# A transformer block on one core: scores in one block ahead of V, tiled half chunks, and two transposes moved from TensorE to DMA

## The chip, the core and the metric

The kernel runs on one core of a Trainium2 chip. The metric is the device time of one execution in microseconds; smaller is better. The core has five engines with queues of their own: TensorE (PE) for matrix products, VectorE (DVE) and ScalarE (ACT) for everything element by element, GpSimd (POOL), and SyncE (SP), which here issues nearly all DMA transfers. Each engine works through its instructions in order; they wait for each other by semaphores.

## The reference, cut to what matters

One diffusion-transformer block: B = 2 sequences of N = 256 tokens, D = 1152 features, two heads of Dh = 576, an MLP of F = 4608.

```python
mod = (silu(c) @ w_mod).reshape(B, 6, 1, D)
shift_a, scale_a, gate_a, shift_m, scale_m, gate_m = [mod[:, i] for i in range(6)]
h = layernorm(x) * (1 + scale_a) + shift_a
q, k, v = (h @ wqkv) split into three, each in H = 2 heads of 576
attn = softmax(q @ k.T * 576 ** -0.5)          # per sequence and head
x = x + gate_a * ((attn @ v) @ wo)
h2 = layernorm(x) * (1 + scale_m) + shift_m
return x + gate_m * (gelu(h2 @ w_fc1) @ w_fc2)
```

## The kernel before

All matrix operands are bf16 and are cut into chunks of 128 rows: D is nine chunks (KD = 9), the 512 tokens are four token tiles t = 0 to 3 (two for each sequence b). A head has 576 = 4.5 chunks, so chunk 4 (HC = 4) is shared: its first 64 rows (HP = 64) belong to head 0, its last 64 to head 1.

The order on each engine is the order in which the program issues its instructions; a loop at its end (L762) pins it. The stages are K, Q, scores and V together, the attention product (PV), the output projection with the second layer norm (Wo), the first MLP product (F1) and the second (F2).

- **Weights.** Every weight matrix of 1152 x 1152 takes one slot of a pool of five (wide, bufs=5), so a load waits until an earlier matrix has been used for the last time. SyncE issues all loads, in program order, mostly in three pieces of 864 KB. In the order of issue: w_scale_a and w_k, w_shift_a, w_q, w_gate_a, w_v, w_shift_m, w_scale_m, w_o, w_f1[0] and w_f1[1] (L121 to L130), then w_f1[2], w_f1[3] and w_gate_mT, the last with three DMA transposes from DRAM (L530 to L537), and during F1 the four parts of w_f2 (L673).
- **Gates.** gate_natural (L410) multiplies silu(c) with w_gate_a during Q (after m = 6), writes the row to DRAM and reads it back with GpSimd's queue, broadcast over the partitions. vec_section makes shift_m and scale_m as columns during V.
- **PSUM.** Accumulators take one of six banks (acc_tile), small results one of two others (aux_tile). `evac` copies a bank to SBUF, in turn on VectorE and ScalarE.
- **Scores.** score_tile (L473) makes one tile of 128 queries by 256 keys in a bank of its own with five matmuls. The shared chunk is multiplied in full: kT4m holds K's chunk 4 twice, each time with the other head's 64 rows set to zero, and v4m does the same for V. reduce_max, Exp with a row sum, reciprocal and a multiplication follow; each of the eight tiles comes ahead of one of the first eight of V's twelve groups (v_group, L503), and its normalization after it.
- **PV.** The attention weights are transposed by 16 TensorE transposes into PSUM (pTt, L546) and copied to SBUF. Then each of nine chunks of each sequence is made by two matmuls, the shared one by four (L567), and copied into aT.
- **Wo and LN2.** wo_group (L629) makes 128 tokens by 384 features, VectorE multiplies with gate_a (tmp), GpSimd adds x into x1, ln2_stats gathers the statistics one group later, and ln2_normalize gives xn2 in bf16 when a token tile is complete. The normalized tiles of a sequence are transposed by 18 TensorE transposes (pt, L605), and on the way out of PSUM VectorE or ScalarE multiply by scale_m and add shift_m into hT. These pieces of work are strewn between other matmuls by `filler`: those of sequence 0 into the last Wo groups, those of sequence 1 into F1.
- **F1** computes m = 0 to 9 for sequence 0, then for sequence 1 (180 matmuls of 256 columns), so that it can begin before sequence 1 is normalized, then m = 10 to 35 for both at once. After m = 14, dot_section makes gate_m with 18 VectorE instructions from w_gate_mT.
- **F2** multiplies 36 chunks for each of 12 groups, VectorE multiplies with gate_m and GpSimd adds x1.

The lines that the steps below speak of:

```python
if m == 6:                                        # L456, in the loop over q
    gate_a = gate_natural(0, w_gate_a)
...
nc.tensor.transpose(                              # L546
    pTt[:, kc, qt * P:(qt + 1) * P],
    attn_tiles[(b, h, qt)][:, kc * P:(kc + 1) * P], ident[:],
)
...
if (t, i) == (3, 0):                              # L654, in the loop over Wo groups
    fill_ln2(0, 5)
```

Of the kernel before, what the change touches and what calls it, by code (L numbers as in the profile page):

```python
# [19 lines left out]
def kernel(  # L20
# [11 lines left out]
    nc = tc.nc  # L32
# [76 lines left out]
    def load_section(name, s):  # L109
        w = wide_tile(name)  # L110
        for r in range(0, KD, 3):
            nc.sync.dma_start(w[:, r:r + 3, :], wmod_v[:, r:r + 3, s * D:(s + 1) * D])
        return w
# [9 lines left out]
    w_gate_a = load_section("w_gate_a", S_GATE_A)  # L123
    w_v = load_panels("w_v", wqkv_v, 2 * D)
    w_shift_m = load_section("w_shift_m", S_SHIFT_M)
    w_scale_m = load_section("w_scale_m", S_SCALE_M)
    w_o = load_panels("w_o", wo_v, 0)
    w_f1 = [None] * 4
    w_f1[0] = load_panels("w_f1_0", wfc1_v, 0)
    w_f1[1] = load_panels("w_f1_1", wfc1_v, D)  # L130
# [10 lines left out]
    kT4m = act.tile([P, H, T], BF16, name="kT4m")  # L141
    v4m = act.tile([P, NT, H, P], BF16, name="v4m")
    nc.gpsimd.memset(kT4m[HP:P, 0, :], 0.0)
    nc.gpsimd.memset(kT4m[0:HP, 1, :], 0.0)
    nc.gpsimd.memset(v4m[:, :, 0, HP:P], 0.0)
    nc.gpsimd.memset(v4m[:, :, 1, 0:HP], 0.0)

# [138 lines left out]
    def k_evac(m):  # L288
        if m == HC:
            evac(kT4m[0:HP, 0, :], pk[m][0:HP, :])  # L290
            evac(kT4m[HP:P, 1, :], pk[m][HP:P, :])
        else:
            evac(kT[:, m, :], pk[m][:])
# [157 lines left out]
    for m in range(KD):  # L451
# [7 lines left out]
        if m == 6:  # L459
            gate_a = gate_natural(0, w_gate_a)  # L460


    def head_chunks(h):
        return list(range(HC + 1)) if h == 0 else list(range(HC, KD))
# [5 lines left out]
    attnT_all = soft[:, 3 * n_s * N:4 * n_s * N].rearrange("p (i c n) -> p i c n", c=TPB, n=N)  # L470
    attn_tiles = {}

    def score_tile(b, h, qt):  # L473
        chunks = head_chunks(h)
        q0 = b * N + qt * P
        ps_s = acc_tile([P, N], "ps_s")
        for i, cc in enumerate(chunks):
            if cc == HC:
                k_ap = kT4m[:, h, b * N:(b + 1) * N]
            else:  # L480
                k_ap = kT[:, cc, b * N:(b + 1) * N]
            nc.tensor.matmul(  # L482
                ps_s[:], qT[:, cc, q0:q0 + P], k_ap,
                start=(i == 0), stop=(i == len(chunks) - 1),
            )
        negmax = small.tile([P, 1], FP32, name="negmax", tag="negmax")
        nc.vector.reduce_max(negmax[:], ps_s[:], axis=AX.X, negate=True)
        si = (b * H + h) * TPB + qt
        e_sb = e_all[:, si, :]
        rowsum = small.tile([P, 1], FP32, name="rowsum", tag="rowsum")  # L490
        nc.scalar.activation(e_sb, ps_s[:], ACT.Exp, bias=negmax[:], scale=1.0, accum_out=rowsum[:])
        attn = attn_all[:, si, :]
        attn_tiles[(b, h, qt)] = attn

        def finish():
            rs = small.tile([P, 1], FP32, name="rs", tag="rs")
            nc.vector.reciprocal(rs[:], rowsum[:])
            nc.vector.tensor_scalar_mul(attn, e_sb, rs[:])

        return finish  # L500


    def v_group(pnl, t):  # L503
# [7 lines left out]
        c4 = HC * P - pnl * PW  # L511
        if 0 <= c4 and c4 + P <= PW:
            evac(v4m[:, t, 0, 0:HP], pacc[:, c4:c4 + HP])
            evac(v4m[:, t, 1, HP:P], pacc[:, c4 + HP:c4 + P])

    score_order = [(b, h, qt) for b in range(B) for h in range(H) for qt in range(TPB)]
    v_order = [(pnl, t) for pnl in range(NPD) for t in range(NT)]
    shift_m = scale_m = None
    for i, (pnl, t) in enumerate(v_order):
        fin = score_tile(*score_order[i]) if i < len(score_order) else None  # L520
        v_group(pnl, t)
        if fin is not None:
            fin()
        if i == 8:
            shift_m = vec_section(sT, w_shift_m, "shift_m")
        if i == 10:
            scale_m = vec_section(sT, w_scale_m, "scale_m")
            nc.vector.tensor_scalar_add(scale_m[:, :, 0:B], scale_m[:, :, 0:B], 1.0)

    w_f1[2] = load_panels("w_f1_2", wfc1_v, 2 * D)  # L530
    w_f1[3] = load_panels("w_f1_3", wfc1_v, 3 * D)
    w_gate_mT = wide_tile("w_gate_mT")
    for r in range(0, KD, 3):
        nc.sync.dma_start_transpose(
            w_gate_mT[:, :, r * P:(r + 3) * P],
            w_mod[r * P:(r + 3) * P, S_GATE_M * D:(S_GATE_M + 1) * D],
        )  # L537


    attnTs = {}  # L540
    for b in range(B):
        for h in range(H):
            pTt = acc_tile([P, TPB, N], "pTt", BF16)
            for qt in range(TPB):
                for kc in range(TPB):
                    nc.tensor.transpose(  # L546
                        pTt[:, kc, qt * P:(qt + 1) * P],
                        attn_tiles[(b, h, qt)][:, kc * P:(kc + 1) * P], ident[:],
                    )
            attnT = attnT_all[:, b * H + h, :, :]  # L550
            evac(attnT, pTt[:])
            attnTs[(b, h)] = attnT

    cpairs = [(0, 1), (2, 3), (4, 5), (6, 7), (8,)]
    for b in range(B):
# [247 lines left out]
```

## Time and profile before

| What | Value |
|---|---|
| median of five runs | 249.05 us (248.59 to 249.12) |
| the profiled execution | 249.12 us |
| its span | 247.3 us |
| granted TensorE clock | 1.0 throughout |
| bytes moved by DMA | 52.18 MB, mean 211 GB/s over the span |
| Q begins, scores and V begin | 33.98 us, 52.77 us |
| pTt transposes begin, PV begins | 77.33 us, 78.23 us |
| Wo begins, F1 begins | 82.76 us, 101.15 us |
| F1 ends, F2 begins | 173.62 us |

A profile is one execution; its span runs from its first to its last recorded instruction, and what lies around the span makes the difference to the execution's time. Times in the trace count from the span's start. In the chain of waits each piece is either work of an engine or a wait, followed back from the last instruction: what stands there is on the path that sets the end. In the rows, L is a line of the kernel above, PE the matmuls, PEld the weight loads that overlap them, SPq the issuing of transfers by SyncE. A number after x is a count of instructions, and the arrow in "out<-in" points from what is read to what is written. Several program tiles share one name in the trace: "big" holds q, k, v and the attention output, "soft" the softmax's three arrays, and "w_f" all parts of the MLP weights.

### The profile page before, as it was taken

To read this page: it belongs to the slowest core of one execution; us is meant where nothing else is said; L and a number is where in the kernel's file an instruction comes from. 1 tells how busy PE (TensorE), PEld (TensorE's weight loads), DVE (VectorE), ACT (ScalarE), POOL (GpSimd) and SP (SyncE) were. 2 spreads that over 40 slices of the span, in tenths; PEclk is the share of its full clock that TensorE was granted. 3 is DMA by queue.
4 is the path that set the end of the run, shared out by engine and by line. 5 is a ranking of instruction groups with operands and counts; after the bars stand their busy time and mean duration, and the time that the engine had idled before them with its cause. 6 is when DMAs were issued, how large, how long until landed. Compare 5 with 4: busy or idle time off the path is not lost.

```text
span 247.3 us, 4011 instructions
## 1 busy us (share of the span) xinstructions
PE 238.7 (97%) x1709; PEld 144.2 (58%) x1709; DVE 88.3 (36%) x209; ACT 68.3 (28%) x133; POOL 34.4 (14%) x53
## 2 busy tenths in 40 slices
PE   6799999999999999989999999999999999999994
PEld 2485444456667766878844444444566666666674
DVE  2761471335544677821099991000011100000001
ACT  6632341153424424593332223322000000000000
POOL 4000021031000166300000003100011122111111
PEclk9999999999999999999999999999999999999999
DMA  6999999999999999999793007999500000000000
GB/s 222 325 333 362 367 330 372 336 362 392 381 328 329 327 328 327 327 292 241 145 321 103 0 3 222 326 342 326 170 16 16 19 16 16 21 16 16 30 21 16
DMA packets 63837, 52.18 MB, mean 211 GB/s; under 512 B 12091, under 2 KB 58571, under 8 KB 63819
## 3 DMA queue, kind: packets, MB, share of 16 engines
q1 hardware_dynamic: 62928, 50.14, 67.0%
q0 software_dynamic: 864, 1.79, 2.1%
q8 instruction: 13, 0.21, 0.4%
q14 instruction: 5, 0.04, 0.1%
q10 hardware_dynamic: 27, 0.00, 0.0%
HBM read 48.08 MB, written 1.19 MB: 199 GB/s over the span
## 4 chain that ended last, share of the span: by engine, by line
PE 90%; DMA 3%; DVE 2%; ACT 2%; issue 1%; SPq 0%; ACTq 0%; DVEq 0%
PE pacc L748 28%; PE pacc L681 26%; PE pacc L506 7%; PE pacc L454 7%; PE pacc L634 7%; PE pk L265 4%; DMA w_scale_a<-in_w_mod_dram 3%; PE pk L298 2%; PE pa L567 2%; PE ps_s L482 2%; PE pn L381 1%; DVE stats L175 1%; PE pt L605 1%; PE pm L233 1%; PE pt L243 1%
## 5 line engine op out<-in xcount | busy, mean ns | idle before, releaser
L681 PE MATMUL pacc<-hT,w_f 128*128 128x512 bf16 (+1 forms) x414 | 71.1, 333 | 0.0
L748 PE MATMUL pacc<-w_f,gT 128*128 128x384 bf16 (+2 forms) x468 | 70.5, 314 | 0.0
L748 PEld LDWEIGHTS <-gT 128*128 128x128 bf16 x468 | 44.4, 98 | 26.2
L681 PEld LDWEIGHTS <-w_f 128*128 128x128 bf16 x414 | 40.3, 98 | 29.4
L754 DVE TENSOR_TENSOR tmp<-pacc,gate 128x384 f32<-128x384 f32 (+2 forms) x13 | 6.8, 526 | 88.3 <-PE pacc L748 88.3
L445 DVE SCALAR_TENSOR_TENSOR late<-w_gate_mT,late 128x1152 bf16<-128x1152 bf16 x18 | 24.4, 1357 | 12.1 <-DMA w_gate_mT<-in_w_mod_dram 11.5
L725 ACT ACTIVATE gT<-pacc 128x512 bf16<-128x512 f32 x26 | 15.5, 597 | 35.0 <-PE pacc L681 35.0
L756 POOL TENSOR_TENSOR o_sb<-tmp,x 128x384 bf16<-128x384 f32 (+1 forms) x12 | 11.7, 972 | 73.3 <-DVE tmp L754 73.3
L506 PE MATMUL pacc<-w_v,hT 128*128 128x384 bf16 x108 | 19.2, 326 | 0.0
L634 PE MATMUL pacc<-w_o,big 128*128 128x384 bf16 x108 | 18.5, 326 | 0.0
L454 PE MATMUL pacc<-hT,w_q 128*128 128x512 bf16 x81 | 17.8, 379 | 0.0
L641 POOL TENSOR_TENSOR x<-tmp,x_sb 128x384 f32<-128x384 f32 x11 | 10.1, 915 | 33.3 <-issue 27.2
L506 PEld LDWEIGHTS <-hT 128*128 128x128 bf16 x108 | 10.4, 98 | 6.3 <-issue 0.5
L634 PEld LDWEIGHTS <-big 128*128 128x128 bf16 x108 | 10.4, 98 | 6.2
L265 PE MATMUL pk<-big,w_k 128*128 128x256 bf16 (+2 forms) x90 | 13.4, 293 | 0.4 <-ACT big L252 0.4
L454 PEld LDWEIGHTS <-w_q 128*128 128x128 bf16 x81 | 7.8, 98 | 9.6 <-issue 0.3
L265 PEld LDWEIGHTS <-w_k 128*128 128x128 bf16 x90 | 7.5, 97 | 3.4 <-DMA w_k<-in_wqkv_dram 0.3
L436 POOL DMA_DIRECT2D gates_dram<-grow x4 | 2.0, 513 | 45.2 <-DVE grow L711 45.2
L284 DVE TENSOR_SCALAR big<-pacc 128x512 bf16<-128x512 f32 x5 | 3.5, 691 | 13.3 <-PE pacc L454 13.3
L640 DVE TENSOR_TENSOR tmp<-pacc,gate 128x384 f32<-128x384 f32 x12 | 6.7, 556 | 3.7 <-PE pacc L634 3.6
L697 ACT ACTIVATE gT<-pacc 128x512 bf16<-128x512 f32 x10 | 5.9, 598 | 7.4 <-PE pacc L681 7.4
L158 PE MATMUL pwarm<-zeros 128*128 128x512 bf16 x19 | 6.5, 486 | 1.2 <-DVE eps_t L92 1.2
(109 smaller groups left out, 171.3 us busy)
## 6 DMA issues: line engine op xcount, KB each, us to landing
w_f<-in_w_fc_dram SPq DMA_DIRECT2D x14, 864.0 KB, 10.2
w_f<-in_w_fc_dram SPq DMA_DIRECT2D x2, 2592.0 KB, 18.4
w_f<-in_w_fc_dram SPq DMA_DIRECT2D x2, 1728.0 KB, 13.4
w_shift_a<-in_w_mod_dram SPq DMA_DIRECT2D x3, 864.0 KB, 10.9
w_q<-in_wqkv_dram SPq DMA_DIRECT2D x3, 864.0 KB, 12.2
w_gate_a<-in_w_mod_dram SPq DMA_DIRECT2D x3, 864.0 KB, 10.2
w_v<-in_wqkv_dram SPq DMA_DIRECT2D x3, 864.0 KB, 12.7
w_shift_m<-in_w_mod_dram SPq DMA_DIRECT2D x3, 864.0 KB, 10.2
```

The costliest lines, as they stand in the source:

```text
L265: nc.tensor.matmul(pk[m][:, c0:c1], w_k[:, k, m * P:(m + 1) * P], hT0[:, k, c0:c1], start=(k == 0 and c0 == 0), stop=(k == KD - 1), skip_g ...
L445: nc.vector.scalar_tensor_tensor(spill, wT[:, j, :], 1.0, s_all[:, b, :], op0=ALU.mult, op1=ALU.mult, accum_out=dst[:, b * KD + j:b * KD + ...
L454: nc.tensor.matmul(pacc[:], w_q[:, k, m * P:(m + 1) * P], hT[:, k, :], start=(k == 0), stop=(k == KD - 1),)
L506: nc.tensor.matmul(pacc[:], hT[:, k, t * P:(t + 1) * P], w_v[:, k, pnl * PW:(pnl + 1) * PW], start=(k == 0), stop=(k == KD - 1),)
L634: nc.tensor.matmul(pacc[:], aT[:, k, t * P:(t + 1) * P], w_o[:, k, c0:c1], start=(k == 0), stop=(k == KD - 1),)
L640: nc.vector.tensor_tensor(tmp[:], pacc[:], gate_a[:, b, c0:c1], op=ALU.mult)
L641: (nc.gpsimd if pool_add else nc.vector).tensor_tensor(x1[:, t, c0:c1], tmp[:], x_sb[:, t, c0:c1], op=ALU.add)
L681: nc.tensor.matmul(dst, w_f1[m // KD][:, k, ml * P:(ml + 1) * P], hT[:, k, c0:c1], start=(k == 0), stop=(k == KD - 1),)
L725: nc.scalar.activation(gT[:, m, :], pacc[:], ACT.Gelu_apprx_tanh)
L748: nc.tensor.matmul(pacc[:], gT[:, kk, t * P:(t + 1) * P], w_f2[j][:, r, c0 - n * PW:c0 - n * PW + cw], start=(kk == 0), stop=(kk == KF - 1),)
L754: nc.vector.tensor_tensor(tmp[:], pacc[:], gate_m[:, b, c0:c0 + cw], op=ALU.mult)
L756: (nc.vector if last else nc.gpsimd).tensor_tensor(o_sb[:], tmp[:], x1[:, t, c0:c0 + cw], op=ALU.add)
```

## The change

1. **Scores.** All eight score tiles are made in one block after Q and ahead of V. The two query tiles of one sequence and head share a bank, so the scores hold four banks. The four full chunks of each head come first (32 matmuls of 256 columns). The shared chunk is then multiplied with only the 64 rows of each head, the matmul placed on the upper or lower half of the array's rows (`tile_position=(h * HP, 0)`), heads in turn. kT4m, v4m and their memsets go.
2. **Softmax** handles both query tiles of a sequence and head at once (one reduce_max over 128 x 2 x 256, two Exp, one reciprocal, two multiplications), ahead of each of V's first four groups.
3. **Attention weights** are transposed by one DMA transpose for each sequence, SBUF to SBUF, on SyncE's queue, in place of pTt and its copies.
4. **PV** multiplies the shared chunk with 64 columns for each head, on the left or right half of the array's columns; it is one PSUM tile for both sequences.
5. **LN2's output** is transposed by one DMA transpose for each token tile, SBUF to SBUF, straight into hT; then ln2_modulate runs nine VectorE instructions in place over hT for a sequence, for sequence 0 behind Wo group (3, 0), for sequence 1 behind the first half of F1. `filler` and the delay of token tile 2's normalization go.
6. **Order of transfers and gate.** w_v is loaded ahead of w_gate_a, gate_natural runs after V's sixth group, both vec_section calls after its eleventh. On SyncE's queue the two attention transposes come ahead of w_o, w_f1[0] and w_f1[1]; the four LN2 transposes come ahead of w_f1[2], w_f1[3] and w_gate_mT.

```diff
     w_q = load_panels("w_q", wqkv_v, 0)
-    w_gate_a = load_section("w_gate_a", S_GATE_A)
+    w_gate_a = wide_tile("w_gate_a")
     w_v = load_panels("w_v", wqkv_v, 2 * D)
+    load_section("w_gate_a", S_GATE_A, w_gate_a)
     w_shift_m = load_section("w_shift_m", S_SHIFT_M)
     w_scale_m = load_section("w_scale_m", S_SCALE_M)
-    w_o = load_panels("w_o", wo_v, 0)
-    w_f1 = [None] * 4
-    w_f1[0] = load_panels("w_f1_0", wfc1_v, 0)
-    w_f1[1] = load_panels("w_f1_1", wfc1_v, D)
...
-    kT4m = act.tile([P, H, T], BF16, name="kT4m")
-    v4m = act.tile([P, NT, H, P], BF16, name="v4m")
...
-        if m == HC:
-            evac(kT4m[0:HP, 0, :], pk[m][0:HP, :])
-            evac(kT4m[HP:P, 1, :], pk[m][HP:P, :])
-        else:
-            evac(kT[:, m, :], pk[m][:])
+        evac(kT[:, m, :], pk[m][:])
...
-        if m == 6:
-            gate_a = gate_natural(0, w_gate_a)
...
+    scores = {}
+    for b in range(B):
+        for h in range(H):
+            scores[b, h] = acc_tile([P, TPB, N], "ps_s")
+            for qt in range(TPB):
+                q0 = b * N + qt * P
+                for i in range(HC):
+                    cc = h * (HC + 1) + i
+                    nc.tensor.matmul(
+                        scores[b, h][:, qt, :], qT[:, cc, q0:q0 + P], kT[:, cc, b * N:(b + 1) * N],
+                        start=(qt == 0 and i == 0), stop=False, skip_group_check=True,
+                    )
+    for b in range(B):
+        for qt in range(TPB):
+            q0 = b * N + qt * P
+            for h in range(H):
+                rows = slice(h * HP, (h + 1) * HP)
+                nc.tensor.matmul(
+                    scores[b, h][:, qt, :], qT[rows, HC, q0:q0 + P], kT[rows, HC, b * N:(b + 1) * N],
+                    start=False, stop=True, skip_group_check=True, tile_position=(h * HP, 0),
+                )
...
+    def attn_transpose(b):
+        n_b = H * TPB
+        nc.sync.dma_start_transpose(
+            attnT_all[:, b, :, :],
+            attn_all[:, b * n_b:(b + 1) * n_b, :].rearrange("p i n -> p (i n)"),
+        )
...
     for i, (pnl, t) in enumerate(v_order):
-        fin = score_tile(*score_order[i]) if i < len(score_order) else None
+        if i < B * H:
+            softmax(i // H, i % H)
+            if i % H == H - 1:
+                attn_transpose(i // H)
         v_group(pnl, t)
-        if fin is not None:
-            fin()
-        if i == 8:
+        if i == 5:
+            gate_a = gate_natural(0, w_gate_a)
+        if i == 10:
             shift_m = vec_section(sT, w_shift_m, "shift_m")
-        if i == 10:
             scale_m = vec_section(sT, w_scale_m, "scale_m")
...
+    w_o = load_panels("w_o", wo_v, 0)
+    w_f1 = [None] * 4
+    w_f1[0] = load_panels("w_f1_0", wfc1_v, 0)
+    w_f1[1] = load_panels("w_f1_1", wfc1_v, D)
...
+    def pv_shared():
+        pa = acc_tile([P, B, TPB, P], "pa")
+        for b in range(B):
+            for kc in range(TPB):
+                for h in range(H):
+                    f0 = HC * P + h * HP
+                    nc.tensor.matmul(
+                        pa[h * HP:(h + 1) * HP, b, :, :], v_sb[:, b * TPB + kc, f0:f0 + HP], attnT(b, h, kc),
+                        start=(b == 0 and kc == 0), stop=(kc == TPB - 1),
+                        skip_group_check=True, tile_position=(0, h * HP),
+                    )
+        evac(aT[:, HC, :], pa[:].rearrange("p b q n -> p (b q n)"))
+
+    pv_chunks(0, 0)
+    pv_chunks(0, 1)
+    pv_shared()
+    pv_chunks(1, 0)
+    pv_chunks(1, 1)
...
+    def ln2_transpose(t):
+        nc.sync.dma_start_transpose(hT[:, :, t * P:(t + 1) * P], xn2[t][:])
+
+    def ln2_modulate(b):
+        for k in range(KD):
+            h = hT[:, k, b * N:(b + 1) * N]
+            nc.vector.tensor_scalar(
+                h, h, scale_m[:, k, b:b + 1], shift_m[:, k, b:b + 1], op0=ALU.mult, op1=ALU.add,
+            )
...
-            if t != NT - 2:
-                ln2_normalize(t, t == NT - 1)
+            ln2_normalize(t, t == NT - 1)
+            ln2_transpose(t)
...
     for o, (t, i) in enumerate(order):
-        if (t, i) == (3, 0):
-            fill_ln2(0, 5)
         wo_group(t, i, o < len(order) - 1)
         if o:
             ln2_stats(*order[o - 1])
-    while fill:
-        fill.pop(0)()
-    ln2_normalize(NT - 2, False)
+        if (t, i) == (NT - 1, 0):
+            ln2_modulate(0)
     ln2_stats(*order[-1])
+
+    w_f1[2] = load_panels("w_f1_2", wfc1_v, 2 * D)
+    w_f1[3] = load_panels("w_f1_3", wfc1_v, 3 * D)
+    w_gate_mT = wide_tile("w_gate_mT")
...
+        if b == 0:
+            ln2_modulate(1)
```

pv_chunks makes the full chunks of one sequence and head, two to a PSUM tile, with the same two matmuls for a chunk as before.

## The prediction

> **What bounds the kernel now.** I read the page's busy and chain parts first, then the chain piece by piece, then SyncE's own timeline for the order of the transfers, then the windows around the DMA transposes that the kernel already has. From the page:
>
> ```profile
> PE 238.7 (97%) x1709; PEld 144.2 (58%) x1709; DVE 88.3 (36%) x209; ACT 68.3 (28%) x133; POOL 34.4 (14%) x53
> ...
> DMA  6999999999999999999793007999500000000000
> ...
> PE 90%; DMA 3%; DVE 2%; ACT 2%; issue 1%; SPq 0%; ACTq 0%; DVEq 0%
> ```
>
> TensorE is busy for 97% of the span. The DMA row says more: the engines are full until about 110 us, then largely free. So TensorE sets the time, but whatever is put on the DMA queues before 110 us stands behind weights. The chain of waits (start, us, what) shows what can go from TensorE:
>
> ```profile
> 52.77 0.55 PE ps_s L482 x5
> ...
> 77.33 0.89 PE pTt L546 x16
> 78.22 0.00 issue
> 78.23 4.53 PE pa L567 x40
> ...
> 96.73 0.22 PE pt L605 x4
> ...
> 108.77 0.92 ACT hT L610 x2
> 109.69 0.04 issue
> 109.73 0.38 PE pt L605 x4
> ...
> 112.19 61.42 PE pacc L681 x334
> 173.62 70.30 PE pacc L748 x468
> ```
>
> The work to be removed is on the path: the pTt and pt transposes, part of the eight ps_s tiles, and a 0.92 us wait of TensorE for ScalarE. SyncE's timeline shows the transfers, issued in program order (start, length of the whole group):
>
> ```profile
> 51.00 4.54 SPq L112 DMA_DIRECT2D w_scale_m<-in_w_mod_dram  x3
> 55.64 13.73 SPq L118 DMA_DIRECT2D w_o<-in_wo_dram  x3
> 69.47 32.37 SPq L118 DMA_DIRECT2D w_f<-in_w_fc_dram  x12
> 101.93 17.78 SPq L534 DMA_TRANSPOSE w_gate_mT<-in_w_mod_dram  x3
> ```
>
> The twelve w_f pieces (864 KB) are issued every 2.7 us and, by the answer for L118, land 10.0 to 10.4 us after issue: nearly four pieces are always ahead of a new one. The sixth (the last of w_f1[1]) is issued at 83.0 and lands at 93.2. A transpose behind it waits that long, however early its data are ready. The windows (PE, PEld, DVE, ACT, POOL, clock, DMA share, GB/s) show a DMA transpose from DRAM alone on the engines:
>
> ```profile
> 113.00:114.00 1.00, 1.00 (x12) 0.88 (x11) 0.00 (x0) 0.60 (x1) 0.00 (x0) 1.00 0.57 127
> 115.00:116.00 1.00, 1.00 (x12) 0.90 (x10) 0.00 (x0) 0.60 (x1) 0.00 (x0) 1.00 1.28 290
> 117.00:118.00 1.00, 1.00 (x11) 0.90 (x10) 0.00 (x0) 0.60 (x1) 0.00 (x0) 1.00 0.65 130
> ```
>
> It moves 290 GB/s with a gap of about a microsecond between two of them; weights moved 326.
>
> [...] here a TensorE block costs 55 ns of the path (0.22 us for four), and no run shows one DMA block alone. [...] The column tiles of L381 agree (36 matmuls in four column groups in 1.22 us, 0.136 us for four side by side); row tiles are not in this trace.
>
> **The change, part by part.** TensorE first.
> Scores: before, 8 x 0.55 = 4.4 us. After, 32 full matmuls at 0.11 (3.5) and four row-tiled pairs. No row prices these: [...] I take 0.13 from the column tiles: 0.5. Gain 0.4 (0 to 0.45).
> pTt transposes: 0.89 goes.
> PV: 4.53 becomes 32 x 0.113 = 3.6 plus four column pairs, 0.5: gain 0.4 (0 to 0.45).
> LN2 transposes: 36 x 0.055 = 2.0, half inside the output projection (Wo), half inside F1, and the 0.92 wait. About 0.3 more of F1's first 11.0 us is neither matmul, transpose nor wait (80 x 0.109 + 1.0 + 1.0 = 10.7) and goes with them.
> gate_natural moves from q to after V's sixth group: 1.2 us on both sides.
> So Wo ends at 101.3 - 0.4 - 0.89 - 0.4 - 1.0 = 98.6, and everything together would give 2.7 + 1.0 + 0.9 + 0.3 = 4.9 us.
>
> Softmax: four serial rounds on VectorE and ScalarE of about 2.6 us (reduce_max over 512 about 0.7, two Exp of 0.57, reciprocal 0.2, two multiplications of 0.27), with V's evacuations between: done 11.5 us after the scores, which end near 55.6, so at 67.1. The score tiles hold four of six PSUM banks; in the built program V's groups take the freed banks in the order in which these rounds release them, each at least 1 us early by this count. No stall; if a round took 4 us, V's fifth group would wait about 2 us.
>
> Attention transposes on SyncE: the first is ready at 61.5, the second at 67.1. w_scale_m, which landed at 68.9 before, lands about 1.5 us sooner (issue 53.3 and 15.6 to landing), since gate's 576 KB broadcast has moved away. Each transpose has 262 KB, 0.9 us at 290 GB/s, plus about 1 us where copies turn into transposes. w_o stands behind both: its data start near 70.3 instead of 68.9. PV needs the attention weights at 76.9: over 4 us of cover. w_o's third piece, landed near 77 before, comes near 79 and is needed at 84. The gate's copies wait behind the softmax on VectorE (67.8), and 15 us later (48.8 to 64 before) it lands near 83, about when the first Wo group wants it; six banks hide 8 us.
>
> w_f1[0] and w_f1[1] inherit 1.6 us from this and 1.8 from the gate's 576 KB, now ahead of them: 93.2 + 3.4 = 96.6. The normalized token tiles 0 and 1 were done at 92.2 and 96.6 (ends of their xn at L594) and come 1.7 us sooner with Wo's start: 90.5 and 94.9. Their transposes stand in the ring behind w_f1[1]: 1 us of turnover and 2 x 1.0 us of data, so both have landed at L = 99.6. Without any queue tile 1 alone would land at 94.9 + X, with X from below, 99.2: the queue and the latency give nearly the same. ln2_modulate(0) is nine VectorE instructions at 0.2 start to start (L402: twelve in 2.44 us): 1.9 us, and the first nine F1 matmuls (1.0) follow one by one, so F1 effectively starts at L + 0.95 = 100.55: TensorE waits 1.95.
>
> The modulate is also a new wait on VectorE: tmp of Wo groups (3,1) and (3,2), the statistics and normalization of tile 3 are queued behind it. From its end: two tmp, add, two stats, aggregate, Sqrt, reciprocal, nb, xn, with the durations of 101.35 to 106.37 before, about 5.1 us. The last transpose is issued at L + 7.0 = 106.6 on an empty queue. No row shows one from SBUF. DRAM ones: 1.8 us from issue to the first data (the 117 window), 1.0 of data, 1 to 2 until the landing: X = 4.3, between 1.6 (an output store of 96 KB) and 6.8 (the fastest w_gate_mT of 884 KB). Landed 110.9; b = 1 of F1 starts effectively at 111.85, while b = 0 ended at 100.55 + 9.8 = 110.35: waits 1.5.
>
> Later: w_f1[2], w_f1[3] and w_gate_mT are issued after 106.6 instead of 85.7 to 102. On empty engines they land by about 126, needed from 134 (m = 18), and 140. The dot products end near 165 instead of 148.7 and gate_m 16 us after them, near 181; the first F2 group ends near 178, and six banks cover 30 us. The last F2 tile waits for the dot products, lands by 183, is needed at 218. All hidden.
>
> Sum: 4.9 - 1.95 - 1.5 = 1.45 us off the profiled execution of 249.12 (span 247.3): 247.7. The median of the runs, 249.05, lies 0.07 lower: 247.6.
>
> **The rivals.** B, nearly all hidden: the ring clears sooner and a landing from SBUF is quick (L = 97.9, X = 3): the first wait falls to 0.25, the second to 0.2: 249.05 - 4.45 = 244.6. For it: a store of 96 KB lands in 1.6 us on a free queue. Against: DMA share 1.1 at 326 GB/s through 106 us, and both numbers have to fall.
> C, slower: a transpose that both reads and writes SBUF runs at half rate. That costs 1.8 on the two attention transposes, 2.0 on tiles 0 and 1 and 1.0 in X, 4.8 in all: 252.4. Place: F1's first wait, and again its second. It decides once L + X passes 99.6 + 4.3 + 1.45 + 0.5 = 105.85. For it: nothing in this trace prices that path. Against: the DRAM transposes' packets are small too (12091 under 512 B on the page) and still run at 290.
> D, the tiles don't do what they say: [...] 0.8 lost, and with a microsecond of L also missed, 249.1.
>
> **How the numbers follow.** Forecast 0.48, B 0.10, C 0.30, D 0.12. The forecast's own range is 245.4 to 249.2 (L and X uncertain by 1.5 and 1). A measurement of this kernel tells 0.2% (0.5 us) from no change. Faster: B and 0.40 of the forecast, 0.50. Same: 0.05 of the forecast and 0.07 of D, 0.12. Slower: C, 0.03 of the forecast and 0.05 of D, 0.38. The range 244.4 to 252.4 leaves out the ends of B and C.
>
> **What would show it.** Wo ending near 98.6; TensorE idle twice, about 2 us before F1 and 1.5 us before its second half, released by VectorE's modulate, which itself waits for a transpose that landed after w_f1[1]. It is wrong if V or PV stalls, if w_o comes late, if the landing of the last transpose is far from 4.3 us, or if F2 waits for gate_m or weights.

## The result and the profile after

The changed kernel takes 249.53 us (median of 29 runs, 248.49 to 252.23), the kernel before 248.86 (49 runs on the same chip): a ratio of 1.0022 with an interval of [1.0012, 1.0032]; the ratio leaves out the one run of 252.23, which was over 1.5% above the fastest. It is slower by 0.7 us where 247.6 had been forecast. Its profiled execution took 250.15 us, with a span of 248.4.

The page of the changed kernel, busy time, DMA row and chain shares:

```profile
PE 238.5 (96%) x1657; PEld 140.6 (57%) x1657; DVE 87.2 (35%) x204; ACT 60.7 (24%) x116; POOL 32.8 (13%) x49
...
DMA  6999999999999999299999999799600000000000
...
PE 86%; DMA 7%; DVE 4%; ACT 1%; issue 0%; SPq 0%; DVEq 0%; ACTq 0%
```

TensorE lost work, but its share of the chain fell from 90% to 86%: DMA rose from 3% to 7% and VectorE from 2% to 4%. The chain of waits says where (start, us, what):

```profile
51.27 3.49 PE ps_s L458 x32
54.76 0.54 PE ps_s L467 x8
...
76.69 1.75 PE pa L535 x16
78.44 0.56 PE pa L547 x8
79.00 1.85 PE pa L535 x16
80.85 14.64 PE pacc L597 x90
95.51 0.38 DVE tmp L602
95.89 3.87 DMA hT<-xn
99.85 0.47 DVE hT L586 x2
100.37 1.88 DVE hT L586 x7
102.25 0.47 DVE tmp L602
...
106.30 0.93 ACT xn L573
107.25 5.16 DMA hT<-xn
112.50 0.36 DVE hT L586
112.90 61.67 PE pacc L649 x324
174.57 70.30 PE pacc L713 x468
```

Up to 80.85 all is as forecast: tiled scores (L467) and tiled PV (L547) take 0.54 and 0.56 us for four pairs each, and Wo begins 1.9 us sooner than before. From 95.5 on the chain has left TensorE for 17 us. It runs over the transpose of token tile 1, the modulate of sequence 0, tile 3's statistics and normalization behind that modulate on VectorE, tile 3's transpose and the first chunk of the second modulate. TensorE's own timeline (start, us, engine, line, what, count, idle before it and what ended the idle):

```profile
99.85 2.40 DVE L586 TENSOR_SCALAR hT<-hT,scale_m,shift_m 128x256 bf16<-128x256 bf16 x9 [2.27 <-DMA hT<-xn]
...
100.25 11.16 PE L649 MATMUL pacc<-hT,w_f 128*128 128x256 bf16 x90 [1.85 <-DVE hT L586]
...
112.90 4.29 PE L649 MATMUL pacc<-hT,w_f 128*128 128x256 bf16 x27 [1.49 <-DVE hT L586]
```

Two waits, 1.85 and 1.49 us, where two were forecast. But the first 90 matmuls take 11.16 us instead of 90 x 0.1083 = 9.75: the first nine follow the modulate one by one (below this is called pacing) and cost 1.4 more. The 27 matmuls at 112.90 take 4.29 us instead of 2.92, for the same reason. F1 ends at 174.57 against 173.62 before; F2 takes 70.3 us in both.

That profile is not the usual execution. The mean granted clock was 0.993 or less in 26 of the 30 runs of the changed kernel, and 1.0 in the profiled one. The kernel before never fell below 0.997.

### The profile page after: what moved, and what is told of

It is laid out like the page before. It is cut to its first block, busy times and chain, and to the rows that moved or that the text cites. A ratio compares the mean times of both kernels' runs of the same rounds, so it can differ in the third digit from the quotient of the medians.

```text
span 248.4 us, 3900 instructions
## 1 busy us (share of the span) xinstructions
PE 238.5 (96%) x1657; PEld 140.6 (57%) x1657; DVE 87.2 (35%) x204; ACT 60.7 (24%) x116; POOL 32.8 (13%) x49
## 4 chain that ended last, share of the span: by engine, by line
PE 86%; DMA 7%; DVE 4%; ACT 1%; issue 0%; SPq 0%; DVEq 0%; ACTq 0%
PE pacc L713 28%; PE pacc L649 25%; PE pacc L503 7%; PE pacc L438 7%; PE pacc L597 6%; PE pk L253 4%; DMA hT<-xn 4%; DMA w_scale_a<-in_w_mod_dram 3%; PE pk L282 2%; PE pa L535 1%; PE pn L365 1%; PE ps_s L458 1%; DVE hT L586 1%; DVE stats L163 1%; PE pm L221 1%; PE pt L231 1%
## 5 line engine op out<-in xcount | busy, mean ns | idle before, releaser
L649 PE MATMUL pacc<-hT,w_f 128*128 128x512 bf16 (+1 forms) x414 | 72.8, 333 | 3.3 <-DVE hT L586 3.3
L503 PE MATMUL pacc<-w_v,hT 128*128 128x384 bf16 x108 | 18.1, 326 | 0.0
L597 PE MATMUL pacc<-w_o,big 128*128 128x384 bf16 x108 | 17.7, 326 | 0.0
L146 PE MATMUL pwarm<-zeros 128*128 128x512 bf16 x19 | 7.5, 549 | 1.2 <-DVE eps_t L92 1.2
L586 DVE TENSOR_SCALAR hT<-hT,scale_m,shift_m 128x256 bf16<-128x256 bf16 x18 | 4.8, 340 | 8.1 <-DMA hT<-xn 8.1
```

The costliest lines, as they stand in the source:

```text
L146: nc.tensor.matmul(dst[:], zeros[:, 0:P], zeros[:], start=True, stop=True)
L503: nc.tensor.matmul(pacc[:], hT[:, k, t * P:(t + 1) * P], w_v[:, k, pnl * PW:(pnl + 1) * PW], start=(k == 0), stop=(k == KD - 1),)
L586: nc.vector.tensor_scalar(h, h, scale_m[:, k, b:b + 1], shift_m[:, k, b:b + 1], op0=ALU.mult, op1=ALU.add,)
L597: nc.tensor.matmul(pacc[:], aT[:, k, t * P:(t + 1) * P], w_o[:, k, c0:c1], start=(k == 0), stop=(k == KD - 1),)
L649: nc.tensor.matmul(dst, w_f1[m // KD][:, k, ml * P:(ml + 1) * P], hT[:, k, c0:c1], start=(k == 0), stop=(k == KD - 1),)
```

## The experiments

T(0) to T(3) are the DMA transposes of the four token tiles. The questions are which half of the change loses, which of the two waits and why, and what the clock does. The first expectations call theory 1 that the loss is all in LN2's half; later ones speak of theory W (only waits) and K (the clock as well). Ratios are against the kernel before, run beside each; differences from the changed kernel or from another experiment compare medians of separate sessions. Each diff is against the changed kernel and is cut. In e4, e5, e6, e7, e10, e11, e15, e16 and e18 the median fell outside every range of time that had been given; what the trace said of the reason stands with each.

### Which half

**e1, the attention half alone**: points 1 to 4 of the change and what goes with them in point 6; LN2 on TensorE with `filler` as before, and w_f1[2], w_f1[3] and w_gate_mT loaded behind w_f1[1].

```diff
-    def ln2_transpose(t):
-        nc.sync.dma_start_transpose(hT[:, :, t * P:(t + 1) * P], xn2[t][:])
+    def ln2_transpose(b, ks, eng):
+        pt = aux_tile([P, len(ks), N], "pt", BF16)
...
```

> The attention half of the change alone (scores in one block, tiled half chunks, attention weights transposed by DMA, the order of loads and of the gate as in the changed kernel up to w_f1[1]); LN2's transposes stay on TensorE as before. Theory 1 (the loss is made in LN2's half): Wo starts 1.9 us sooner as in the trace of the changed kernel (80.85 against 82.76), nothing takes it back: 248.9 - 1.9 = 247.0. Theory 2 (the DMA transposes of the attention weights and the moved loads cost later what the block saves): 248.5 or more.

Measured 247.23 us, 0.9933 [0.9921, 0.9945]: 1.6 us gained, of a forecast 0.4 + 0.89 + 0.4 = 1.7.

**e2, LN2's half alone**: point 5 on the attention of before; of the loads, only those of w_f1[2], w_f1[3] and w_gate_mT stand behind the LN2 transposes.

```diff
-    def attn_transpose(b):
...
+                    nc.tensor.transpose(
+                        pTt[:, kc, qt * P:(qt + 1) * P],
```

> The LN2 half alone (each token tile transposed by DMA on SyncE's queue ahead of w_f1[2], scale and shift in place on VectorE); attention, its order of loads and its gate as before. Theory 1: this half costs what the changed kernel lost plus what its attention half gained, 0.7 + 1.9 = 2.6: about 251.3, with TensorE idle before each half of F1. Theory 2: no loss by itself, 247 to 249.

Measured 248.88 us, 1.0002 [0.9984, 1.0019]. Theory 1 missed: alone the LN2 half costs nothing. Gains of 1.6 and 0 make a loss of 0.7 together. In e2 Wo begins at 82.57, so T(0) is issued at 92.0, with only the tail of w_f1[1] ahead of it (whose last piece lands at 93.0), and T(1) lands in 3.2 us at 99.6; in the changed kernel Wo begins 1.7 us sooner and T(1) lands at 99.76. The attention half's gain ends as idle time ahead of F1.

**e4, sequence 0 on TensorE, sequence 1 by DMA:**

```diff
-            ln2_transpose(t)
+            if t >= TPB:
+                ln2_transpose(t)
...
+        if (t, i) == (3, 0):
+            fill_ln2(0, 5)
```

> The changed kernel with sequence 0 of LN2 transposed on TensorE in the last Wo groups, as before, and only sequence 1 by DMA (token tiles 2 and 3). Theory 1: F1 starts with no wait at about 99.5, tile 3 is normalized by 104, its transpose lands by 109, before F1's first half ends at 109.3: no second wait of more than 1 us, 245 to 246. Theory 2 (DMA transposes late for F1 whatever the order): 248.5 or more.

247.27 us, 0.9930 [0.9917, 0.9943], level with e1 and between the two theories: T(3) took 5.0 us, and TensorE waited twice, 0.57 and 0.50 us, for the evacuation of transposes, since tile 2's normalization stood between them. **e8** puts that behind, moves the late broadcast to SyncE and splits sequence 1's modulate:

```diff
+    ln2_normalize(NT - 2, False)
+    ln2_transpose(NT - 2)
     ln2_stats(*order[-1])
```

> The run with sequence 0 transposed on TensorE and sequence 1 by DMA, with three mendings: token tile 2's normalization is put behind sequence 0's pieces again, the late broadcast is on SyncE's queue behind w_f1[3], and sequence 1's modulate is split between VectorE (five) and ScalarE (four). In its profile TensorE lost 0.57 and 0.5 us in Wo's last groups and the transpose of tile 3 took 5.0 us. If these are the price of that arrangement, Wo ends near 99.8 (18 transposes of 0.055 behind 98.5), the second half of F1 finds its data with no wait over 0.3 us, and the time is 245.5 to 246.5, below the attention half alone (247.23). If tile 3's chain behind the pieces is too late in any case (it lands after 110.5), TensorE waits about 1 us before the second half and the time stays near 247.

246.30 us, 0.9899 [0.9884, 0.9913], as the first of the two cases had it.

### The two waits

**e3**: the late broadcast of silu(c) (2 x 288 KB, which GpSimd issued at 104.77, 2.5 us ahead of T(3)) on SyncE behind w_f1[3].

```diff
+        nc.sync.dma_start(s_all[:, b, :], s_dram[b:b + 1, :].partition_broadcast(P))
...
-        nc.gpsimd.dma_start(s_all[:, b, :], s_dram[b:b + 1, :].partition_broadcast(P))
```

> The changed kernel with the broadcast of silu(c) into late issued on SyncE behind w_f1[3] instead of on GpSimd, where it starts at 104.8 and shares the engines with the last LN2 transpose. Theory 1: the last transpose lands in about 3.2 us as the third did on free engines (5.2 before), TensorE's second wait is 1.5 to 2 us shorter: 247.6 to 248. Theory 2 (5 us is what a transpose from SBUF takes): 249.5, unchanged.

249.44 us, 1.0019 [1.0008, 1.0029]: nothing gained. Yet in its profile T(3) landed in 3.3 us and the second wait was gone; instead the clock was at 0.5 for 3.4 us after the first wait of 1.93 us.

**e6**: four of nine modulates on ScalarE.

```diff
+            if k % 2 == 0:
                 nc.vector.tensor_scalar(
...
+            else:
+                nc.scalar.activation(
+                    h, h, ACT.Identity, bias=shift_m[:, k, b:b + 1], scale=scale_m[:, k, b:b + 1],
```

> The changed kernel with the odd four of the nine modulate instructions of each sequence on ScalarE, five left on VectorE; the second sequence's are issued ahead of the last Gelu of the first half. If the size of the modulate is what my sum had wrong (nine instructions in 2.40 us instead of 1.8), nine now take about 1.4 us: TensorE's F1 starts about 0.9 us sooner in effect, tile 3's chain on VectorE is 1 us shorter, and the second half starts about 1 us sooner again: 247.6 to 248.2. If the landings of the transposes decide alone, the two waits end only with the first modulated chunk and not more than 0.5 us is gained: 249.0 to 249.5. Under theory K, a first stretch of F1 that runs less paced also loses fewer half-clock stretches, so up to 1 us more than the first figure.

248.57 us, 0.9988 [0.9976, 1.0]: 1.0 us below the changed kernel, and between the ranges given. The four runs at full clock (247.74 to 248.51) lie about where the modulate theory put them; ten of 14 had the half clock.

**e9**: e3 and e6 together.

> The changed kernel with both terms of my sum mended at once: the modulate split between VectorE and ScalarE, and the late broadcast on SyncE's queue behind w_f1[3], out of the way of tile 3's transpose. By the sum, F1 still waits 1.9 us for token tile 1, its first nine matmuls are paced by 0.4 us instead of 1.2, and the second half finds its data: F1 ends near 98.4 + 1.9 + 0.4 + 71.2 = 171.9 instead of 174.57, and the execution takes 247.5. Theory W (waits alone): the median is 247.2 to 247.8. Theory K (where the second wait is gone, the half-clock stretch behind the first wait is no longer covered by it and costs its full 1.7 us): most runs show a clock of 0.993 and the median is 248.4 to 249.2, while runs at clock 1.0 are near 247.5.

248.47 us, 0.9984 [0.9971, 0.9997]. The six runs at full clock have a median of 247.6, as the mended sum says; the 16 others 248.7. So theory K fits here, at about 1.1 us.

**e5 and e10**: 14 dummy matmuls into the changed kernel's two waits, and nine into the first wait of e9.

```diff
     ln2_stats(*order[-1])
+    warm(8, aux_tile([P, T], "pwarm3"))
...
             ln2_modulate(1)
+            warm(6, aux_tile([P, T], "pwarm3"))
```

> The changed kernel with 14 more matmuls of 512 columns on zeros, whose results nothing reads: eight (0.216 us each, 1.73 us) between Wo and F1, six (1.30 us) between the two halves of F1's first part. They fill TensorE's two waits and should not lengthen them (1.85 and 1.49 us in the profile of the changed kernel). Theory W (the time went only into waits of TensorE for transposes and for VectorE's modulate): the median stays within 0.4 us of the changed kernel's 249.5 and the runs spread as widely as before, over 1.5 us. Theory K (beside the waits, a TensorE that idles and then runs paced is granted half its clock for a stretch of 3.4 us in some executions, as in the profile of the run with the late broadcast, where it cost about 1.7 us): the median falls by 0.5 to 1.5 us, to 248.0 to 249.0, and the runs stay within about 1 us of each other.

> The same with nine matmuls of 512 columns on zeros between Wo and F1 (1.94 us), which nothing reads; they fill the first wait and lengthen it by 0.2 us at most. Theory K: the clock stays at 1.0 in nearly all runs, and the median is 247.3 to 247.9, about 1 us or more below the run without them. Theory W: the same time as without them or up to 0.2 us more.

The half clock all but goes (one run of 20, against 42 of 52 of the changed kernel and e9), but the times are 250.18 us (1.0062 [1.0045, 1.0079]) and 248.88 (1.0000 [0.9989, 1.0011]): neither theory has them. In e5 the six dummies before the second half outlasted its data by about 0.4 us, and 250.2 is what the changed kernel's own full-clock runs take (249.75 to 250.15). In e10's profile T(3) took 4.8 us, against 3.3 in e9's. A full clock gains nothing when T(3) is late. The two runs also differ in more than the clock: dummies are TensorE instructions, and they brought an instruction fetch of TensorE into T(3), from 110.1 to 108.7 us (its part is told below). So these two runs don't price the half clock.

**e13**: the changed kernel once more.

> The changed kernel once more, for a second profile of it: 25 of its 30 runs have a mean clock of 0.993 or less, while its profile has 1.0. If the half-clock stretch follows the first wait and takes the place of the second, as in the run with the late broadcast moved, this profile shows a clock near 0.5 for 3.4 us between 101 and 107, no wait of TensorE before the second half of F1 (or one below 0.4 us), and F1's end within 0.7 us of 174.57. If the stretch comes on top of both waits, F1 ends 1.7 us later than 174.57. With a clock of 1.0 it tells nothing of this.

249.46 us, clock 0.993. Its windows (busy PE, PEld, DVE, ACT, POOL; then the granted clock, DMA share, GB/s) and TensorE's timeline:

```profile
100.00:102.00 2.00, 0.97 (x4) 0.49 (x5) 1.37 (x6) 0.00 (x0) 0.00 (x0) 0.83 0.79 148
102.00:104.00 2.00, 2.00 (x10) 1.07 (x9) 2.00 (x7) 0.00 (x0) 0.43 (x1) 0.50 0.00 0
104.00:106.00 2.00, 2.00 (x17) 1.61 (x16) 1.93 (x5) 0.00 (x0) 0.94 (x2) 0.81 0.00 0
```

```profile
101.03 16.21 PE L649 MATMUL pacc<-hT,w_f 128*128 128x256 bf16 x124 [2.43 <-DVE hT L586]
```

Half the clock for 2 x (0.17 x 2 + 0.5 x 2 + 0.19 x 2) = 3.4 us, which costs 1.7 us of TensorE; then 124 matmuls with no second wait. F1 ends at 173.85. The stretch takes the second wait's place. By its clock of 0.993 that is the usual execution of the changed kernel, and it would explain why taking away the second wait's supposed cause (e3) gained nothing.

The profiles of the kernel before and of the changed kernel record the clock at 1.0 from 6.07 to 248.41 and from 7.75 to 250.09, and at 0.5 from there: 242.35 us in both, 71 times 3.413, whatever the waits between. By the windows of e3, e6 and e13 the half clock lasted 3.4 us in each, one such step. Ahead of it stood 2.43 us of idle and the first two of nine paced matmuls in e13, and a wait of 1.93 us in e3. The half clock goes with how much of one step TensorE works, counting a matmul of 256 columns as 0.108 us: the 3.413 us ahead of the half clock in e3, e6, e7 and e13 were filled for 0.17 to 0.21, and the last step at 1.0 in the profiles of before and after holds no matmul. The least filled step ahead of that one in the changed kernel's profile, from 243.27 (0.40), was followed by full clock, and so was the one from 110.15 (0.41). In the same profile a step ends at 99.91 (7.75 + 27 x 3.413), in the middle of the first wait, which leaves 0.51 and 0.55 on its two sides. In e9's profile a wait of 2.16 us brought no half clock either (mean clock 1.0). So length alone doesn't decide: 1.85 and 2.16 us passed, 1.93 and 2.43 did not. That it is where a wait lies in these steps is my reading of the changed kernel's profile.

### The queue ahead of the transposes

The answers for the changed kernel's T(0) (issue time in ns, landing in us):

```profile
L581 SPq DMA_TRANSPOSE hT<-xn x1: 5427/5427/5427, 90.4 to 90.4; - x1
...
DMA to landing us min/median/max: 8.4/8.4/8.4
```

T(0)'s issue holds SyncE for 5.4 us behind w_f1[1]. T(1), whose tile was ready at 94.64, is issued only at 95.89. **e7** takes the load of w_f1[1] from its old place and puts it behind T(1):

```diff
+            if t == TPB - 1:
+                for n in range(NPD):
+                    nc.sync.dma_start(
+                        w_f1[1][:, :, n * PW:(n + 1) * PW], wfc1_v[:, :, D + n * PW:D + (n + 1) * PW]
+                    )
```

> The changed kernel with the load of w_f1[1] issued behind the transposes of token tiles 0 and 1 instead of ahead of w_o's end; it is first needed at m = 9, near 109 us. If the ring is what keeps tile 1's landing at 99.76 although its tile was normalized at 94.64, it now lands 3.2 to 3.5 us after that, near 98.1, and F1's first matmul follows near 98.7 instead of 100.25: 1.5 us gained at the first wait. w_f1[1]'s three pieces (8 us of transfers) are through by 106, so that tile 3's transpose stays near 3.5 to 5 us; its issue moves with the modulate. Total 247.5 to 248.5. If latency and turnover of the transposes set the landing (the other reading in my prediction, that queue and latency give nearly the same), tile 1 lands no sooner than 99.3 and the time stays at 249.2 to 249.8, or is worse where w_f1[1] now comes late at m = 9.

251.14 us, 1.0082 [1.0069, 1.0096]. Its chain:

```profile
94.64 3.26 DMA hT<-xn
...
98.00 2.39 DVE hT L586 x9
...
105.39 6.74 DMA hT<-xn
```

T(1) lands at 97.9 and the first wait is gone: the ring (SyncE's queue of transfers) was its cause. T(0) took 8.4 us from issue to landing behind w_f1[1] and takes 3.2 here. But T(2) and T(3) now stand behind w_f1[1], T(2) takes 10.1 us, T(3) 6.74, TensorE waits 3.07, and half the clock follows from about 113.96 on (mean clock 0.993). **e11** moves only the last two pieces, and behind T(3):

```diff
+    load_f1_1(0)
...
     ln2_stats(*order[-1])
+    load_f1_1(1)
+    load_f1_1(2)
     w_f1[2] = load_panels("w_f1_2", wfc1_v, 2 * D)
```

> The changed kernel with two of the three pieces of w_f1[1] (those for m = 12 to 17, needed from about 120 us) issued behind the transpose of tile 3 instead of ahead of the transpose of tile 0. Unlike the run with the whole of w_f1[1] behind tile 1, nothing but transposes is on SyncE's queue from tile 0 to tile 3. If the ring sets tile 1's landing, it lands near 98.0 (94.64 + 3.3), the first wait is at most 0.1 us, the chain of tile 3 moves with the modulate to an issue near 105.5, it lands by 110 behind the late broadcast, and F1's second half starts 2.4 us sooner than in the changed kernel: 247.0 to 247.8, about what I had forecast. If latency sets the landing, 249.2 to 249.8.

248.26 us, 1.0001 [0.9985, 1.0016]: by the median 1.3 us below the changed kernel, by the mean (248.80 against 249.58) 0.8, since there are two groups: 12 runs at full clock with a median of 248.1, 10 at 0.993 with 249.6. There is no first wait, but a second of 1.39 us remains: T(3), issued at 105.45, took 5.05. With the split and the late broadcast's move as well (**e12**), and with each alone (**e14**, split; **e15**, broadcast):

> The same two pieces behind tile 3, with the split modulate and the late broadcast on SyncE's queue too. Sum: no first wait, pacing 0.4 us, tile 3's transpose issued near 104.5 and landed near 107.8 while the first half runs to 108.8: F1 ends near 98.4 + 0.1 + 0.4 + 71.2 = 170.1, and the execution takes 245.4 to 246.0, at or below the best hybrid (246.30), and with no idle no half-clock stretch: clock 1.0 and runs within 0.5 us. If something else of the transposes by DMA costs time (the later loads of w_f1, w_gate_mT), it stays above 246.5.

> The two pieces of w_f1[1] behind tile 3 and the split modulate; the late broadcast stays on GpSimd's queue. The run with the two pieces alone had 248.26, that with all three mendings 246.03, so 2.2 us are left for the split and the broadcast. If the modulate is the term (0.8 us of pacing at each half and 1 us of tile 3's chain), tile 3's transpose is issued near 104.3 and landed by 108 to 109.3 even beside the broadcast, at the time the first half ends (108.9): 246.0 to 246.8. If the broadcast is (tile 3's transpose in 5 us instead of 3.3), TensorE still waits over 1 us before the second half and some runs show the half clock: 247.2 to 248.2.

> The two pieces of w_f1[1] behind tile 3 and the late broadcast on SyncE's queue; the modulate stays on VectorE alone. If the broadcast is the term, tile 3's transpose (issued 105.4) lands near 108.8, the first half ends at 109.6, there is no second wait and no half clock: 246.2 to 246.8. If the modulate is, the first nine matmuls of each half stay paced by it (1.2 us each) and a transpose of 4.8 us still brings a wait in some executions: 247.0 to 248.0.

e12: 246.03 us, 0.9889 [0.9876, 0.9902]. e14: 246.16, 0.9891 [0.9875, 0.9907]. e15: 248.67, 0.9991 [0.9972, 1.001]. By the medians the split is worth 2.1 us there and the broadcast nothing: with it out of the way T(3) still took 5.1 us. So the broadcast, which I had taken for the cause of the slow T(3) since e3, is not. Part of what the split gains is T(3) itself, issued 1.5 us sooner and landed in 3.8 us.

### What makes the last transpose slow

Laid beside each other, the profiles part by one thing. An instruction fetch (one packet of 16 KB on queue q8, which the page calls "instruction"; 0.9 to 1.4 us in the changed kernel's profile) starts inside T(3) in the changed kernel (at 109.7) and in e2, e4, e5, e8, e10, e11 and e15, and T(3) takes 3.9 to 5.2 us (in e7 6.7, beside the copies). In e3, e6, e9, e12, e13 and e14 it starts after T(3) has landed (in e9 0.1 us before that), and T(3) takes 3.3 to 3.8: 3.3 where the broadcast is out of the way (e3, e9, e12), 3.6 to 3.8 beside it (e6, e13, e14), so the broadcast costs a little after all. In the changed kernel's profile q8 has 13 such packets, and 178 to 316 of TensorE's 3314 instructions (1657 matmuls, 1657 weight loads) start between two of them. If it is TensorE that fetches, matmuls added at the start should move the fetch. **e16** replaces the 14 long matmuls of the warm-up at the start of e11 by 54 short ones, **e17** does so with e14:

```diff
-    warm(14, pwarm)
+    for _ in range(54):
+        nc.tensor.matmul(pwarm[:, 0:P], zeros[:, 0:P], zeros[:, 0:P], start=True, stop=True)
```

> The run with two pieces of w_f1[1] behind tile 3 (248.26, tile 3's transpose 5.05 us), in which the 14 matmuls of 512 columns that warm TensorE at the start are replaced by 54 of 128 columns, about the same time for TensorE there. In the fifteen profiles so far, tile 3's transpose took 3.3 to 3.8 us where no instruction fetch (a 16 KB packet on the queue of kind instruction, about 1.1 us) fell between its issue and its landing, and 3.9 to 5.2 (6.7 behind w_f1[1]) where one did. Theory F (the fetch holds the transpose up): 40 more matmuls ahead should bring TensorE's fetch of 108.2 some 4 us forward, to near 104, ahead of the transpose's issue at 105.5; it lands in 3.3 to 3.9 us, the second wait of 1.39 us falls below 0.4, no half clock follows, and the median is 246.8 to 247.5. Rival (the fetch is not TensorE's, or only comes along with the slow transposes): the transpose stays near 5 us and the median near 248.3.

> The same 54 short matmuls in the run with the two pieces moved and the modulate split (246.16, tile 3's transpose 3.8 us from 103.9, fetch at 110.9). Theory F: if the fetch comes some 4 us sooner, near 106.5, it falls into the transpose, which then takes 4.5 to 5.2 us and lands near 108.7; the first half ends near 109, so that TensorE hardly waits, and the median is 246.2 to 246.9. Rival: the transpose stays at 3.3 to 3.8 us.

e16: 246.50 us, 0.9906 [0.9890, 0.9922], 1.8 us below e11 (1.6 below e11's runs at full clock) and no half clock in six runs. The DMA answers from T(3)'s issue to its landing, e11's first, then e16's:

```profile
q1 hardware_dynamic: 1489, 0.53, 74.5%
q0 software_dynamic: 104, 0.35, 18.5%
q8 instruction: 1, 0.02, 1.1%
...
hT<-xn SPq DMA_TRANSPOSE x1, 5.1
```

```profile
q1 hardware_dynamic: 1218, 0.32, 58.1%
q0 software_dynamic: 101, 0.34, 26.6%
...
hT<-xn SPq DMA_TRANSPOSE x1, 3.5
```

The same 0.34 MB of the broadcast (q0) passes in both; the fetch is absent in e16 (it came at 102.4 instead of 108.2, with nothing changed but TensorE's instructions), T(3) lands in 3.5 us and F1's first 153 matmuls run without a wait. F1's start was also some 0.3 us sooner, so the fetch's part is about the second wait of 1.39 us that is gone. In e17 the fetch came at 104.5, 0.4 us after T(3)'s issue: 4.2 us instead of 3.8, and 246.23 us (0.9889 [0.9875, 0.9903]), since the first half covers it. That is a weak test of the way back. A fetch inside is also not enough by itself: T(0) in e11 and e14 had one that began 0.2 and 0.4 us after the issue, in e12 one that began 0.15 ahead of it, and landed in 3.2, 3.4 and 3.6 us (3.2 without one, in e16). One that began 0.9 us after T(3)'s issue came with 3.9 us (e2), those that began 1.7 to 3.0 us after it with 4.8 to 5.2 (the changed kernel, e4, e10, e11, e15, e18). So in these profiles the later starts go with the slower transposes.

**e18** takes the pacing from e14: the first four columns of each half run chunk by chunk, and ScalarE has chunks 4, 6 and 8.

```diff
+        for k in range(KD):
+            for m in range(4):
+                nc.tensor.matmul(
+                    firsts[m // 2][:, m % 2, :], w_f1[0][:, k, m * P:(m + 1) * P], hT[:, k, b * N:(b + 1) * N],
```

> The run with the two pieces moved and the modulate split (246.16), with the first four columns m of each half of F1 multiplied chunk by chunk (k outside, m inside: four matmuls, 0.43 us, for each modulated chunk) and with ScalarE given only chunks 4, 6 and 8, since it is still busy with tile 2's normalization at 97.5 to 98.7. In the profile without this, TensorE waits 1.02 us for ScalarE's chunk 1 and is paced by it until 100.70, some 1.8 us behind a start without pacing. If pacing is all that is left, the first half is 1.2 to 1.8 us sooner and the median 244.5 to 245.2, limited by tile 3's transpose, which then may end after the first half. If tile 3's transpose, issued near 104.2 and landed near 107.9 at best, sets the time instead, TensorE waits for it at the first half's end near 107.9 and the median is 245.2 to 246.0.

246.29 us, 0.9886 [0.9868, 0.9905]. The first half now runs in 10.0 us, but the fetch fell into T(3) at 106.8, it took 5.0 us, and the gain went into that wait, in the timeline:

```profile
110.10 4.09 PE L672 MATMUL pacc<-hT,w_f 128*128 128x256 bf16 x36 [1.74 <-DVE hT L592]
```

e8, e12, e14, e16, e17 and e18 all lie at 246.0 to 246.5, below both kernels; they are not told apart here.

## Why the prediction was wrong

By its own steps, against the profiled execution (250.15 forecast as 247.7):

- Scores, PV, softmax, attention transposes, Wo's end: right. Scores took 3.49 + 0.54 us, PV 4.16, the attention weights were ready at 60.8 and 66.2 without a stall, Wo's end at 98.40 against 98.6. e1 bears out the whole half.
- L = 99.6: measured 99.76. The sentence beside it was wrong: without any queue tile 1 lands at 97.9 (e7) or 98.0 (e11), not 99.2, since X is 3.2 to 3.3 there.
- **The modulate, "nine VectorE instructions at 0.2 start to start": mis-sized.** That row was an addition with one column of scalars. With two, in place, nine take 2.40 us, 0.26 start to start, and the first matmul comes 0.4 after the first. F1 effectively started at L + 1.90 instead of L + 0.95. The first half ended at 111.41 instead of 110.35, T(3) was issued at 107.25 instead of 106.6, and the second nine were paced too.
- **X = 4.3: 5.16 measured.** One number stood for two cases, 3.3 to 3.8 without an instruction fetch inside and 3.9 to 5.2 with one.
- The second half's effective start is thus late by 0.16 (L) + 0.49 (modulate in tile 3's chain) + 0.86 (X) + 0.91 (first chunk and pacing) = 2.42 us, with 2.4 found at F1's end (174.57 against 173.62 - 1.45). Of this the modulate makes 1.4.
- That the idle times, 1.85 and 1.49, are so near the forecast 1.95 and 1.5 is luck. Those figures contained the pacing; with it TensorE lost 3.26 and 2.86 us.
- Not in the sum at all: the half clock after the first wait. In most runs, if e13's profile is typical, it takes the second wait's place, so that either mending alone brings little.
- Later loads, w_gate_mT, gate_m, F2: hidden, as forecast. The DMA row of before was misread, without consequence: it is full to 117 us, busy to 130 and again from 148 to 179.

Rival C had the right sign and the wrong reason. Its threshold, L + X past 105.85, was not reached (99.76 + 5.16 = 104.92), and while T(3) passed on a free ring in e3, from 108.5 to 110.0, the DMA engines moved 168 to 217 GB/s, where half of the DRAM transposes' 290 is 145. B's figures, L = 97.9 and X = 3, are about what a free ring without a fetch gives (98.0 in e11, 3.3 in e3); this kernel's order of loads doesn't leave the ring free. D, which had the row and column pairs one after the other, fell: four pairs take 0.54 and 0.56 us, 0.14 a pair, where a full matmul takes 0.11. Together, the two pieces of w_f1[1] moved and the modulate split (e14) turn the change from 0.7 us slower to 2.7 faster.

Open: why e3's runs at full clock (249.62 to 250.48) are slower than its others. A fetch inside T(3) would do it, but no profile caught such a run. Open too is by what way a fetch of about 1 us holds up a transpose on another queue by more than 1 us.

## What to carry to other kernels

A stage that starts earlier gains only if everything that its successor waits for moves too. List what stands in the DMA ring and on each engine ahead of the last input, and move first what is needed last. Price a chain element by the same form of instruction, count the pacing of the first consumers as well as the wait, and allow for half the clock over another 3.4 us when TensorE waits about 2 us and then runs paced (1.93 us in e3, 2.43 in e13; 26 of the changed kernel's 30 runs had a mean clock of 0.993 or less). Look where an instruction fetch falls (T(3) took 5.05 us with one inside in e11, 3.5 without in e16) before blaming a transfer beside a slow one.

## What was unexpected of the hardware

- The granted clock went to half for 3.4 us (e3, e6, e13) after 3.413 us that TensorE filled for 0.17 to 0.21, and stayed full after 0.40 and 0.41 in the changed kernel's profile. In the profiles of e3, e6 and e13 the half clock came after a wait of 1.9 to 2.4 us, while the first matmuls ran paced; 26 of the changed kernel's 30 runs had a mean clock of 0.993 or less. The kernels without a wait over 1.1 us in their profiles (e1, e2, e4, e5, e8, e10, e12, e14, e16, e17) had such a clock in 2 of 66 runs, and e18, with 1.74 us of waiting but no pacing, in none of 5.
- One instruction fetch of 16 KB inside a DMA transpose of 288 KB went with a landing 1.6 us later (e11 against e16); about the start of a transpose it went with 0 to 0.4 us more (T(0) in e11, e12 and e14). 40 matmuls at the start of the kernel moved it, 100 us later, by 5.8 us.
- SBUF to SBUF, a transpose of 128x1152 bf16 held SyncE's queue for 1.24 to 1.3 us and landed in 3.2 to 3.3 us on a free ring (T(0) and T(1) in e7, T(2) and T(3) in e3); behind 2.6 MB of copies its issue held SyncE for 5.4 us, with all that stood behind it (T(0) in the changed kernel).
